# The output projection of the second attention stage in half arrays, its loads and stores by GpSimd, and a new order of its steps

## The chip, the cores and the metric

The kernel runs on one core of a Trainium2 chip. A core has a matrix engine (TensorE, PE in the profile; its weight loads are PEld), VectorE (DVE), ScalarE (ACT), GpSimd (POOL) and SyncE (SP), which here only issues DMA transfers. Time is the device time of one execution in microseconds, the median of several runs.

## The reference: what is computed

A sequence of 2048 tokens of width 576 passes through two layers, and each layer is an attention block and a gated mixer block, both with a residual connection:

```python
x = x + _A_ref(_layernorm(x), A_wqkv, A_wo)
x = x + _B_ref(_layernorm(x), B_w_in, B_w_sp, B_b_sp, B_w_out)
```

and the same two lines once more with the same weights. The attention has 32 heads of width 18; a token attends to eight tokens, itself and those 2, 4, ... 14 positions before it. Its result goes through the output projection `A_wo` (576 x 576), which this case is about. The mixer computes `z = gelu(x @ w_in)` of width 4608, normalises the second half (called z2 here) over its width, mixes it over the tokens with `w_sp` (2048 x 2048), adds a bias, multiplies by the first half (z1) and projects back with `w_out`. Inputs and output are bf16.

## The kernel before

The program runs five phases: F (attention of layer one, and z2 of its mixer), S (token mixing), F again (first the output projection of the first mixer, called p3, then the attention of layer two and its z2), S again, and E (the last output projection). The second F is `phase_F` with `first` false; in it TensorE, VectorE, ScalarE, GpSimd and SP work on many small steps side by side.

The tokens are worked on in 16 blocks of 128 rows (index i) for p3, W and z2, in 18 attention tiles of 114 rows (index t), since a tile of 128 keys serves 114 queries, and in six groups of three tiles (index g) for Q and K. The steps of the second F are:

- `p3_steps`: for block i, 36 matmuls (L491) with `w_out`, the residual sum on VectorE (L536), and LayerNorm (`ln_steps`): statistics on VectorE (L416, L417), three small steps on GpSimd (L421 to L424), normalisation on ScalarE (L437), and a transposing DMA on SP into `xnD` (L454).
- `QK_steps`, `V_steps`: projections of Q and K (L395, L401, L720), which SP's DMAs write into `QK`, and of V (L754).
- `ATT_steps`: for tile t, logits (L792), exponential on ScalarE (L799), mask on VectorE (L806), the product with V (L814), the division by the sum on VectorE (L822, L823) into `o_t`, a transposing DMA on SP (`turned`, L849), and a copy into `oT` by VectorE or ScalarE (`ev`, L471 or L472). `o_t` has two buffers.
- `W_steps`: for block i, the output projection of the attention (L880), the residual sum (L536), the store of the row block to DRAM, and the LayerNorm before the mixer, the steps called y.
- `Z2_steps`: the z2 part of `w_in` for block i (L914 and L921 on TensorE), gelu on ScalarE (L937), sums of squares and normalisation on VectorE (L949, L988). Its weights come by ten DMAs, the steps `win2.k`, made in `win2_parts`.

Width 576 is four chunks of 128 rows and 64 more. The contraction over these 64 is done in two ways. `mm576` (L387) runs eight full matmuls for two results and then, or before them, two matmuls of 64 rows, one in the upper and one in the lower half of the array, with the operands lying on partitions 0 to 63 for the one and 64 to 127 for the other. Q and K and z2 work like that. The output projection instead takes five chunks for each half of its columns, where the fifth is filled with zeros: in the second F `o_tb` has 64 columns of zeros behind the 576, and rows 64 to 127 of the last chunk of `wo` are zeros, both written by GpSimd in `fill`.

Nobody writes the order of the steps by hand. Each step is registered with `fl.step(name, engine, cost, key, function, after, uses, takes, mode, pairs)`. `Flow.order` then plays the engines with these costs: of the steps that could begin first on an engine it takes the one with the lowest key. Keys are made of the tile or block number and the numbers in `PLANS`: KX ranks p3, KQ the projections of Q and K, KV those of V, KL the logits, KE the exponentials, KM the masks, KP the product with V, KF the division, KO the transposing DMA of `o_t`; KY ranks the LayerNorm after W, KZ and KS rank z2 (KZ + KS times the block). STAY is a bonus for staying in the same mode. A mode is the way that TensorE's array is divided: "w" full, "n" halves of 64 rows, "c" and "h" halves of columns, "q" quarters of rows; "wn" begins with the one in which TensorE is and ends in the other. The plan thus fixes the order on every engine before the kernel starts, and on the chip each engine works through its list in order and waits on semaphores.

Row stores and z2 weight loads go to the queue that is named `side`, L586:

```python
side, SIDE = (nc.gpsimd, ("POOL", 0.66)) if first else (nc.sync, ("SP", 0.5))
```

A load `win2.k` may be issued when the logits of tile 11 + k // 2 have been given to TensorE and all p3 blocks are through (L1108).

Of the kernel before, what the change touches and what calls it, by code (L numbers as in the profile page):

```python
# [20 lines left out]
P = 128  # L21
HP = 64
S = 2048
D = 576
FH = 2304
H = 32
# [14 lines left out]
NM = D // P  # L41
# [11 lines left out]

Plan = namedtuple("Plan", "LX LW LR KQ KX KV KL KE KM KP KF KY KZ KS STAY LF KO", defaults=(0,))
PLANS = (Plan(LX=4, LW=3.41, LR=2.6, KQ=3.82, KX=5.34,
              KV=1.52, KL=21.62, KE=163.6, KM=20.74, KP=31.25, KF=55.71, KY=7.57, KZ=169.61, KS=25.3, STAY=1.61, LF=4.38, KO=17.77),
         Plan(LX=5.14, LW=3.5, LR=2.6, KQ=6.48, KX=9.99,
              KV=3.68, KL=12.54, KE=0, KM=0, KP=11.94, KF=53.62, KY=74.68, KZ=0, KS=32.42, STAY=8.78, LF=3.89, KO=6.42))
SCALE = DH ** -0.5


# [208 lines left out]
class K:  # L270
# [270 lines left out]
    def phase_F(self, li):  # L541
        nc, tc = self.nc, self.tc
        first = li == 0
# [10 lines left out]
        pl = PLANS[0 if first else 1]  # L554
        fl = Flow(dict(QK=NQK[ly], stg=NSTG[ly], stx=NSTX[ly], xt=NX, xn=3, ln_st=6, o_t=2, oq=2), pl.STAY, self.pairs, pl.LF,
                  0.8 if first else 0.0, first)
# [9 lines left out]
        wo = att.tile([P, 5, D], bf16, name="wo")  # L566
# [4 lines left out]
        oT = att.tile([P, 5, RING], bf16, name="oT")  # L571
        o_tb = [att.tile([P, D if first else D + HP], bf16, name=f"o_t{k}") for k in range(2)]
        oq = [self.zu[:, 0, a:a + 5 * P].rearrange("p (c n) -> p c n", n=P) for a in (0, 2176)]

        def x_tile(i):
            if i < NXZ:
                return self.zu[:, NB, D * i:D * (i + 1)]
            return xts[i - NXZ][:]
# [4 lines left out]
        def x_held(i):  # L583
            return [b for _, b in x_takes(i)]
        win2a = self.wA[:].rearrange("p (c s t) n -> p c s (t n)", c=NM - 1, s=2)
        side, SIDE = (nc.gpsimd, ("POOL", 0.66)) if first else (nc.sync, ("SP", 0.5))  # L586
        win2b = wB[:]
        win2r = wC[:]

# [61 lines left out]
        def load_o():  # L651
            eng = nc.sync
            self.dma(wo[:, 0:4, :], self.A_wo[0:512, :].rearrange("(c p) n -> p c n", p=P), eng)
            self.dma(wo[HP:P, 4, :] if first else wo[0:HP, 4, :], self.A_wo[512:576, :], eng)

# [117 lines left out]
        def ATT_steps(t, key):  # L775
            v, box, Psb = vb[t % 3], {}, Pb[t % 2]
# [3 lines left out]
            tag = f"a{t}"  # L780
# [37 lines left out]
            def fin(_):  # L818
                o_t = box["o"] = o_tb[t % 2][:, 0:D]
                O = box["O"][:, :, 0:16 * (DH + 1)].rearrange("p s (h e) -> p s h e", e=DH + 1)  # L820
                rec = att.tile([P, 2, 16], f32, name="rec", bufs=2)
                nc.vector.reciprocal(out=rec[:], in_=O[:, :, :, DH])  # L822
                nc.vector.tensor_tensor(out=o_t.rearrange("p (s h d) -> p s h d", s=2, d=DH), in0=O[:, :, :, 0:DH],  # L823
                                        in1=rec[:, :, :, None].to_broadcast([P, 2, 16, DH]), op=ALU.mult)
            landed = [f"qk{group[t]}.w{d}" for d in range(NM // 2 + 1)] + ([f"qk{group[t]}.h"] if group[t] else [])
            both = [("H", tag + ".L0"), ("H", tag + ".L1")]
            if first:
# [2 lines left out]
            else:  # L830
                fl.step(tag + ".L", "PE", 0.62, key - pl.KL, lambda _: Lm(0, True), landed, [f"QK{group[t]}"], takes=both, mode="q", pairs=2 * H)
            fl.step(tag + ".x0", "ACT", 0.9, key - pl.KE, ex(0), [tag + (".M" if first else ".L"), "fill"] + ([f"a{t - 2}.v"] if t > 1 else []), [tag + ".L0"],
                    mode="x")
            fl.step(tag + ".x1", "ACT", 0.9, key - pl.KE, ex(1), [tag + ".x0"], [tag + ".L1"], mode="x")
            fl.step(tag + ".k", "DVE", 1.07, key - pl.KM, mk, [tag + ".x1", "masks"])
            fl.step(tag + ".v", "PE", 0.54 if first else 0.53, key - pl.KP, pv, [tag + ".k", f"v{t}.e0", f"v{t}.e1"] + ([f"ones{t}"] if t < 3 else []) + ([f"a{t - 1}.v"] if t else []),
                    takes=[("H", tag + ".O")], mode="c", pairs=H)
            fl.step(tag + ".f", "DVE", 1.11, key - pl.KF, fin, [tag + ".v"], [tag + ".O"], takes=[("o_t", f"o_t{t}")])
            n = min(QT, S - QT * t)

            def tr(_):
# [27 lines left out]
        def W_steps(i):  # L869
            box, g, rows = {}, f"w{i}", slice(P * i, P * i + P)  # L870
            t_of = range(P * i // QT, min(NT - 1, (P * i + P - 1) // QT) + 1)
            key = t_of[-1]
            at = P * i % RING

            def wm(hh):
                def f(_):
                    if hh == 0:
                        box["ps"] = self.Ht()
                    for c in range(5):
                        nc.tensor.matmul(box["ps"][:, hh, 0:288], lhsT=oT[:, c, at:at + P],  # L880
                                         rhs=wo[:, c, hh * 288:(hh + 1) * 288], start=(c == 0), stop=(c == 4))
                return f

            def add(_):
                self.add_x(x_tile(i), box["ps"], x_tile(i))

            def store(_):
                self.dma(self.xres[0 if first else 1][rows, :], x_tile(i), side)
            fl.step(g + ".m0", "PE", 0.61, key, wm(0), [f"a{t}.e" for t in t_of] + ["wo", "fill"], takes=[("H", g + ".ps")], mode="w", pairs=5)
            fl.step(g + ".m1", "PE", 0.61, key, wm(1), [g + ".m0"], [g + ".ps"], mode="w", pairs=5)  # L890
            fl.step(g + ".a", "DVE", 0.73, key, add, [g + ".m1", ("lnx" if first else "p3_") + f"{i}.n"], [g + ".ps", *x_held(i)])
            fl.step(g + ".w", *SIDE, key, store, [g + ".a"], x_held(i), lag=pl.LW)
            users = [t for t in range(NT) if QT * t - HALO < P * (i + 1) and P * i < QT * t + QT]
            guard = [f"v{t}.m" for t in users]
            guard += [f"qk{gg}.m{d}" for gg in sorted({group[t] for t in users}) for d in range(5)]
            self.ln_steps(fl, f"y{i}", key + pl.KY, P * i, lambda: x_tile(i), [g + ".a"], x_held(i), guard)
# [140 lines left out]
        def fill(_):  # L1037
            for k in range(2):
                nc.gpsimd.memset(Pb[k][:, :, :, QH:HP], 1.0)
            nc.gpsimd.memset(wo[0:HP, 4, :] if first else wo[HP:P, 4, :], 0.0)  # L1040
            if not first:
                for k in range(2):
                    nc.gpsimd.memset(o_tb[k][:, D:], 0.0)

        def ones(k):
            def f(_):
# [20 lines left out]
        if first:  # L1067
            fl.step("wv", "SP", 1.4, -18, lambda _: load_v(), lag=6.0)
        fl.step("wo", "SP", 0.9, -17, lambda _: load_o(), ["wv", "qk1.w1"] if first else [], lag=4.0)
        z = "DVE" if first else "POOL"  # L1070
        zero = nc.vector if first else nc.gpsimd
# [4 lines left out]
        for k in range(3):  # L1076
            fl.step(f"vzero{k}", z, 0.6, -4 if first else -12, lambda _, k=k: zero.memset(vbi[k][:], 0), ["lnx1.p"] if first else [])
            fl.step(f"ones{k}", "POOL", 0.5, -3 if first else -15, ones(k), [f"vzero{k}"])
        fl.step("fill", "POOL", 1.5, -40, fill)
        fl.step("masks", "POOL", 2.0, -16, lambda _: self.masks() if first else None)  # L1080
        if first:
# [8 lines left out]
            for k, (n, cost, pre) in enumerate(((9, 5.15, []), (3, 0.95, ["lnx0.t", "spin0"]), (2, 0.6, ["lnx1.t", "spin1"]))):  # L1090
                fl.step(f"spin{k}", "PE", cost, -100, turn(n), pre, ["spin"] if k else [],
                        takes=[] if k else [("H", "spin")], mode="w", pairs=n)
        for i in range(NS):
            g = next(g for g in range(len(sizes)) if QT * (t0s[g] + sizes[g]) > P * i)
# [6 lines left out]
        for t in range(NT):  # L1101
            V_steps(t, t - pl.KV)
        for t in range(NT):
            ATT_steps(t, t)
        for i in range(NS):
            W_steps(i)
# [6 lines left out]
        if first:  # L1113
            made = [f"wqk{b}" for b in range(NM)] + [f"ends{k}" for k in range(4)] + ["wqk_r", "wv"]
# [807 lines left out]
```

## Time and profile before

| what | us |
|---|---|
| median of 3 runs | 1105.55 (1104.48 to 1106.67) |
| profiled execution, its time | 1105.93 |
| its span, first to last instruction | 1104.2 |
| first F, about | 0 to 200 |
| first S | 200 to 489 |
| second F | 489 to 749 |
| second S and E | 749 to 1104 |

The mean clock that TensorE was granted is 0.998 of full speed. The answers of the profile that are quoted below have these forms. A row of a stretch lists its length, then the busy time and number of instructions of PE, PEld, DVE, ACT and POOL, the granted clock, the mean busy share of the 16 DMA engines, and GB/s. A row of waits reads: who waited, for whom, us in total, times, the longest. A row of the order of time begins with start and duration in us; in square brackets stands how long the engine had been idle before it, and what ended that. A group has its count behind an x, then busy us and the mean ns of one. A row of one line's instructions has minimum, median and maximum ns. SPq is an issue on SP's queue; a DMA row ends with the us from issue to landing.

### The profile page before, as it was taken

To read this page: it belongs to the slowest core of one execution; us is meant where nothing else is said; L and a number is where in the kernel's file an instruction comes from. 1 tells how busy PE (TensorE), PEld (TensorE's weight loads), DVE (VectorE), ACT (ScalarE), POOL (GpSimd) and SP (SyncE) were. 2 spreads that over 40 slices of the span, in tenths; PEclk is the share of its full clock that TensorE was granted. 3 is DMA by queue.
4 is the path that set the end of the run, shared out by engine and by line. 5 is a ranking of instruction groups with operands and counts; after the bars stand their busy time and mean duration, and the time that the engine had idled before them with its cause. 6 is when DMAs were issued, how large, how long until landed. Compare 5 with 4: busy or idle time off the path is not lost. (4 is left out here: it accounts for less than half of the span.)

```text
span 1104.2 us, 24979 instructions
## 1 busy us (share of the span) xinstructions
PE 1088.9 (99%) x10249; PEld 621.8 (56%) x10249; DVE 801.6 (73%) x1442; ACT 518.2 (47%) x744; POOL 231.9 (21%) x456
## 2 busy tenths in 40 slices
PE   8999999999999999999999999999999999999998
PEld 5777655444444444457777765554444444444586
DVE  8898888987777677854566788467766676676686
ACT  7788898832221422202465578873122214323250
POOL 6354548411111001122111124530000000000000
PEclk9999999999999999999999999999999999999999
DMA  7877580587769625573344496602122192211421
GB/s 190 169 143 167 133 177 1 150 204 247 226 199 335 207 84 158 165 249 93 73 73 79 95 187 151 245 1 61 36 60 60 40 358 67 60 49 57 175 81 54
DMA packets 192586, 147.96 MB, mean 134 GB/s; under 512 B 145784, under 2 KB 174584, under 8 KB 188760
## 3 DMA queue, kind: packets, MB, share of 16 engines
q1 hardware_dynamic: 182616, 105.92, 37.7%
q0 software_dynamic: 9856, 40.45, 11.1%
q8 instruction: 80, 1.31, 0.5%
q14 instruction: 34, 0.28, 0.1%
HBM read 77.78 MB, written 37.92 MB: 105 GB/s over the span
## 5 line engine op out<-in xcount | busy, mean ns | idle before, releaser
L1303 ACT ACTIVATE zu<-psum 128x1024 bf16<-128x1024 f32 x72 | 73.3, 1021 | 332.9 <-PE psum L1299 292.3
L1318 PE MATMUL psum<-S,T 128*128 128x512 f16 x856 | 198.8, 379 | 0.0
L1318 PEld LDWEIGHTS <-T 128*128 128x128 f16 x1144 | 111.9, 98 | 125.8 <-issue 0.2
L1370 DVE SCALAR_TENSOR_TENSOR g<-psum,wsc,bsp 128x512 f32<-128x512 f32 (+1 forms) x130 | 97.4, 750 | 83.8 <-PE psum L1318 82.4
L1291 PE MATMUL psum<-xnD,w 128*128 128x512 bf16 x576 | 136.4, 380 | 0.0
L914 PE MATMUL psum<-wA,xnD 128*128 128x384 bf16 x576 | 109.7, 327 | 0.3 <-DVE v_ext L471 0.2
L1318 PEld LDWEIGHTS <-zu 128*128 128x128 bf16 x640 | 62.6, 98 | 73.0 <-issue 0.5
L914 PEld LDWEIGHTS <-xnD 128*128 128x128 bf16 x768 | 72.0, 98 | 56.0 <-issue 11.9
L1291 PEld LDWEIGHTS <-w 128*128 128x128 bf16 x576 | 53.4, 98 | 71.1 <-issue 15.3
L1370 DVE SCALAR_TENSOR_TENSOR g<-psum,wsc,g 128x512 bf16<-128x512 f32 (+1 forms) x93 | 66.0, 710 | 36.3 <-PE psum L1318 34.5
L937 ACT ACTIVATE zu<-psum 128x768 bf16<-128x768 f32 x96 | 76.9, 804 | 22.5 <-PE psum L921 20.0
L1318 PE MATMUL psum<-A,zu 128*128 128x512 bf16 x352 | 82.0, 379 | 0.0
L949 DVE CUSTOM_DVE_ANT_1 zu<-zu 128x1536 bf16<-128x1536 bf16 x28 | 49.1, 1752 | 27.1 <-ACT zu L937 26.7
L799 ACT ACTIVATE P<-psum 128x912 bf16<-128x912 f32 x72 | 64.0, 942 | 9.4 <-PE psum L792 6.6
L1318 PE MATMUL psum<-S,zu 128*128 128x512 f16 x288 | 68.0, 379 | 0.3 <-DVE g L1370 0.3
L1318 PE MATMUL psum<-A,T 128*128 128x512 bf16 x288 | 68.0, 379 | 0.0
L401 PE MATMUL psum<-xnD,wqkv 128*128 128x228 bf16 (+1 forms) x480 | 64.9, 280 | 2.3 <-DVE wqkv L623 1.5
L491 PEld LDWEIGHTS <-zu 128*128 128x128 bf16 x576 | 56.1, 98 | 14.7
L1330 DVE TENSOR_TENSOR zu<-g,zu 128x512 bf16<-128x512 bf16 x129 | 54.9, 425 | 8.7
L401 PEld LDWEIGHTS <-wqkv 128*128 128x128 bf16 x480 | 43.7, 97 | 16.7 <-issue 7.6
L437 ACT ACTIVATE xn<-zu,ln_st 128x512 bf16<-128x512 bf16 (+1 forms) x52 | 31.1, 647 | 46.4 <-POOL ln_st L424 46.2
L491 PE MATMUL psum<-wA,zu 128*128 128x288 bf16 x384 | 52.6, 286 | 0.0
(209 smaller groups left out, 1786.4 us busy)
## 6 DMA issues: line engine op xcount, KB each, us to landing
w<-in_B_w_in_dram SPq DMA_DIRECT2D x72, 128.0 KB, 2.5
ustore<-zu POOLq DMA_DIRECT2D x18, 512.0 KB, 3.6
zu<-ustore SPq DMA_DIRECT2D x18, 512.0 KB, 4.2
S<-op SPq DMA_DIRECT2D x8, 1024.0 KB, 13.8
A<-op SPq DMA_DIRECT2D x6, 1024.0 KB, 11.1
wA<-in_B_w_out_dram SPq DMA_DIRECT2D x12, 432.0 KB, 4.2
QK<-stg SPq DMA_DIRECT2D x36, 114.0 KB, 3.9
QK<-stg SPq DMA_DIRECT2D x24, 171.0 KB, 3.7
```

What stands on the lines that cost most here:

```text
L401: nc.tensor.matmul(ps(s), lhsT=lhsT, rhs=rhs, start=(c == 0 and not rest_first), stop=(c == NM - 1 and rest_first))
L437: nc.scalar.activation(out=out, in_=in_, func=ACT.Identity, scale=rstd[:n], bias=nmr[:n])
L491: nc.tensor.matmul(ps[:, hh, 0:288], lhsT=u[:, s * S + i * P:s * S + (i + 1) * P], rhs=wout(b, s)[:, hh * 288:(hh + 1) * 288], start=(b == ...
L799: nc.scalar.activation(out=Psb[:, 2 * hh:2 * hh + 2, :, 0:QH], in_=box["L", hh][:, :, 0:8 * QH].rearrange("p a (b c) -> p a b c", c=QH), f ...
L914: nc.tensor.matmul(box[u][:, s, 0:384], lhsT=self.xnD[:, c, at], rhs=(win2a[:, c, s] if c < NM - 1 else win2b[:, s])[:, cols], start=(firs ...
L937: nc.scalar.activation(out=self.zu[:, 3 * u + 1:3 * u + 4, 256 * i:256 * (i + 1)].rearrange("p j (s r) -> p s j r", s=2), in_=box[u][:, :, ...
L949: nc.vector.tensor_tensor_reduce(out=junk(0, 6), in0=z[:, 0:6, :], in1=z[:, 0:6, :], scale=1.0 / FH, scalar=0.0, op0=ALU.mult, op1=ALU.add ...
L1291: nc.tensor.matmul(ps[:, h, :], lhsT=w1[:, NM * h + d, :], rhs=self.xnD[:, d, t0:t0 + 512], start=(opens and d == 0), stop=(not opens and ...
L1303: nc.scalar.activation(out=u_of(jj, c)[:, :, 512 * k:512 * k + 512], in_=ps, func=ACT.Gelu_apprx_tanh)
L1318: nc.tensor.matmul(ps, lhsT=lhs[:, i, :], rhs=rhs[:, i, :], start=(opens and i == 0), stop=(i == 7), skip_group_check=not opens)
L1330: nc.vector.tensor_tensor(out=uv, in0=g, in1=uv, op=ALU.mult)
L1370: nc.vector.scalar_tensor_tensor(out=out, in0=ps, scalar=inv[c], in1=other, op0=ALU.mult, op1=ALU.add)
```

## The change

It has four parts, all in the second F; the first F keeps its form.

1. The output projection of a block becomes one step in the manner of `mm576`: eight full matmuls and two of 64 rows in the two halves of the array (`halves`), with mode "wn". For this the last 64 rows of `wo` are loaded twice, to both halves of the partitions (`load_o`), and VectorE copies the last 64 columns of `o_t` behind the 576 (`fin`), so that the transposing DMA delivers them on both halves. The zeros in `fill` go.
2. The row stores and the z2 weight loads are issued by GpSimd instead of SP (`side`).
3. The costs in the plan follow: 1.1 for W as one step, 1.21 for the division with the copy.
4. The numbers of the second plan are new, and so the order of all steps of the second F.

```diff
-         Plan(LX=5.14, LW=3.5, LR=2.6, KQ=6.48, KX=9.99,
-              KV=3.68, KL=12.54, KE=0, KM=0, KP=11.94, KF=53.62, KY=74.68, KZ=0, KS=32.42, STAY=8.78, LF=3.89, KO=6.42))
+         Plan(LX=5.14, LW=3.5, LR=2.6, KQ=6.06, KX=9.99, KV=2.42, KL=11.66, KE=10.56, KM=-1.95, KP=11.34, KF=71.99, KY=260.04, KZ=0, KS=0.84, STAY=8.35, LF=3.89, KO=0.46))
...
-        side, SIDE = (nc.gpsimd, ("POOL", 0.66)) if first else (nc.sync, ("SP", 0.5))
+        side, SIDE = nc.gpsimd, ("POOL", 0.66)
...
-            self.dma(wo[HP:P, 4, :] if first else wo[0:HP, 4, :], self.A_wo[512:576, :], eng)
+            for k in (1,) if first else (0, 1):
+                self.dma(wo[HP * k:HP * k + HP, 4, :], self.A_wo[512:576, :], eng)
...
+                if not first:
+                    nc.vector.tensor_copy(out=o_tb[t % 2][:, D:D + HP], in_=o_t[:, D - HP:D])
...
-            fl.step(tag + ".f", "DVE", 1.11, key - pl.KF, fin, [tag + ".v"], [tag + ".O"], takes=[("o_t", f"o_t{t}")])
+            fl.step(tag + ".f", "DVE", 1.11 if first else 1.21, key - pl.KF, fin, [tag + ".v"], [tag + ".O"], takes=[("o_t", f"o_t{t}")])
...
+            def halves(rest_first):
+                ps = box["ps"] = self.Ht()
+                cols = [slice(288 * hh, 288 * hh + 288) for hh in range(2)]
+                self.mm576(lambda hh: ps[:, hh, 0:288], rest_first,
+                           lambda hh, c: (oT[:, c, at:at + P], wo[:, c, cols[hh]]),
+                           lambda hh, rows: (oT[rows, NM, at:at + P], wo[rows, NM, cols[hh]]))
...
-            fl.step(g + ".m0", "PE", 0.61, key, wm(0), [f"a{t}.e" for t in t_of] + ["wo", "fill"], takes=[("H", g + ".ps")], mode="w", pairs=5)
-            fl.step(g + ".m1", "PE", 0.61, key, wm(1), [g + ".m0"], [g + ".ps"], mode="w", pairs=5)
+            made = [f"a{t}.e" for t in t_of] + ["wo"]
+            if first:
+                fl.step(g + ".m0", "PE", 0.61, key, wm(0), made + ["fill"], takes=[("H", g + ".ps")], mode="w", pairs=5)
+                fl.step(g + ".m1", "PE", 0.61, key, wm(1), [g + ".m0"], [g + ".ps"], mode="w", pairs=5)
+            else:
+                fl.step(g + ".m1", "PE", 1.1, key, halves, made, takes=[("H", g + ".ps")], mode="wn", pairs=10)
...
-            nc.gpsimd.memset(wo[0:HP, 4, :] if first else wo[HP:P, 4, :], 0.0)
-            if not first:
-                for k in range(2):
-                    nc.gpsimd.memset(o_tb[k][:, D:], 0.0)
+            if first:
+                nc.gpsimd.memset(wo[0:HP, 4, :], 0.0)
```

## The prediction

> **What bounds the kernel now.** I read the page first, then the busy times by stretch, then who TensorE waited for, and last the order of time around its longest wait.
>
> ```profile
> span 1104.2 us, 24979 instructions
> PE 1088.9 (99%) x10249; PEld 621.8 (56%) x10249; DVE 801.6 (73%) x1442; ACT 518.2 (47%) x744; POOL 231.9 (21%) x456
> ```
>
> TensorE is busy 99% of the span, so only two things can shorten the kernel: less TensorE work, or less of the 1% in which it stands still or runs at a lower clock. The second attention stage (first L491 matmul at 489.44, last z2 matmul at about 749) is the only stage whose order the change touches.
>
> ```profile
> core 0: us, PE busy (x) PEld busy (x) DVE busy (x) ACT busy (x) POOL busy (x), PEclk, DMA share, GB/s
> 489.40:537.00 47.60, 47.60 (x375) 35.88 (x374) 19.26 (x39) 10.46 (x18) 16.59 (x41) 1.00 0.44 112
> 537.00:600.00 63.00, 62.40 (x1135) 45.14 (x1133) 40.72 (x67) 36.55 (x54) 9.81 (x26) 1.00 0.35 69
> 640.00:650.00 10.00, 10.00 (x228) 6.58 (x233) 8.69 (x18) 7.39 (x12) 2.42 (x6) 1.00 0.91 199
> 656.00:658.00 2.00, 2.00 (x51) 1.62 (x51) 1.64 (x4) 1.40 (x3) 0.13 (x1) 1.00 1.46 33
> 658.00:662.00 4.00, 1.94 (x25) 0.83 (x26) 1.66 (x3) 2.01 (x4) 0.00 (x0) 0.86 0.87 175
> 662.00:666.00 4.00, 4.00 (x146) 2.94 (x146) 2.80 (x9) 3.18 (x5) 1.05 (x3) 0.72 0.70 173
> 700.00:749.00 49.00, 49.00 (x320) 26.08 (x318) 29.03 (x39) 36.97 (x85) 16.59 (x39) 1.00 0.19 54
> 489.00:749.00 260.00, 254.84 (x3585) 171.23 (x3584) 164.48 (x277) 157.46 (x281) 74.15 (x172) 0.99 0.49 114
> ...
> PE psum L880 <- ACT oT L472: 2.1, 1, 2.1
> ```
>
> Over the whole stage (the last stretch) TensorE stands still for 260.00 - 254.84 = 5.2 us, with nothing of it before 537 or after 700. The longest wait, 2.1 us on the copy into oT by ScalarE (L472), is followed by a lower clock. The third number from the right is the granted clock: 1.94 x (1 - 0.86) + 4.00 x (1 - 0.72) = 0.27 + 1.12 = 1.4 us is lost there. So 5.2 + 1.4 = 6.6 us is the most that fewer waits can win, and more than half of it (2.1 + 1.4) hangs on one wait. Its causes, in order of time:
>
> ```profile
> 651.28 2.12 SPq L286 DMA_DIRECT2D wA<-in_B_w_in_dram  x2
> 653.50 1.23 SPq L849 DMA_TRANSPOSE zu<-o_t  x1
> 655.58 2.44 SPq L849 DMA_TRANSPOSE zu<-o_t  x1
> 659.94 0.74 ACT L472 COPY oT<-zu 128x570 bf16<-128x570 bf16 x1 [2.54 <-DMA zu<-o_t]
> 660.01 0.76 DVE L823 TENSOR_TENSOR o_t<-psum,rec 128x576 bf16<-128x576 f32 x1 [1.86 <-DMA zu<-o_t]
> 660.73 1.30 PE L880 MATMUL psum<-wo,oT 128*128 128x288 bf16 x5 [2.06 <-ACT oT L472]
> ...
> DMA to landing us min/median/max: 2.6/2.8/3.8
> wA<-in_B_w_in_dram SPq DMA_DIRECT2D x2, 288.0 KB, 5.4
> ```
>
> Two z2 weight loads go out on SP at 651.28, the transposing DMA of an attention output right behind them at 653.50. The median of such a transpose (L849) is 2.8 us to landing; this one is read only at 659.94, which is 6.4 us. Meanwhile ScalarE, VectorE and then TensorE stand still. The two loads, issued on the same queue, needed 5.4. In 656 to 658 the DMA engines are counted as more than fully busy (1.46) while they move 33 GB/s. So the wait is a transfer queued behind others, not arithmetic.
>
> **The change part by part.** *The output projection (W).* TensorE now does ten matmuls for a block of 128 rows, five row chunks for each of two column halves, the fifth chunk padded with zeros. After the change there are eight full ones and two of 64 rows, which lie in two halves of the array.
>
> ```profile
> 578.71 2.61 PE L880 MATMUL psum<-wo,oT 128*128 128x288 bf16 x20 [0.32 <-ACT v_ext L472]
> 581.16 1.63 PE L491 MATMUL psum<-wA,zu 128*128 128x288 bf16 x12
> ...
> 710.93 1.15 PE L914 MATMUL psum<-wA,xnD 128*128 128x384 bf16 x6
> 712.24 1.14 PE L914 MATMUL psum<-wA,xnD 128*128 128x384 bf16 x6
> 714.94 0.66 PE L921 MATMUL psum<-wC,xnD 64*128 64x384 bf16 x6
> 715.53 1.15 PE L914 MATMUL psum<-wA,xnD 128*128 128x384 bf16 x6
> ```
>
> Twenty W matmuls (two blocks) take 581.16 - 578.71 = 2.45 us, so one takes 0.1225 and a block 1.225. The price of the new form is read from z2, which has it already: eight full matmuls take 712.24 - 710.93 = 1.31 us, or 0.164 each. From 710.93 to 715.53 there are 24 of them and three pairs of halves. If a pair takes the time of one full matmul, that is 27 x 0.164 = 4.42; measured are 4.60, and the 0.18 left are two changes between full and half rows, some 0.09 each. So a new W block takes 9 x 0.1225 = 1.10, and 0.09 for the change inside it: 1.19 against 1.225, a gain of 0.035, or 16 x 0.035 = 0.55 us in all. That holds where a block stands between steps of other forms, as in nearly all of the present order, and for two blocks in a row. Bounds: between neighbours that already end and begin in half rows, no extra change is paid, 16 x 0.1225 = 2.0 us gained; a lone block between two full-row steps pays two, 16 x (0.18 - 0.1225) = 0.9 us lost. I take 0.4 gained, nearest to the middle case.
>
> The Trainium skill, TensorEngine Tiling (Array Packing), Key Properties, says that a change of tiling mode drains TensorE, which speaks against this edit; its speedup table would by itself give up to 2x on the last chunk. By the table alone the gain would be 2.0, by the rows above it is 0.55; the 0.09 us per change is what the drain costs here.
>
> *The copy of the last 64 columns.* It replaces a fill with zeros, since the halves need the last 64 rows of the transposed output on both halves of the partitions: 18 copies of 128x64 on VectorE, between the division (L823) and the transposing DMA.
>
> ```profile
> L471 DVE COPY oT<-zu 128x60 bf16<-128x60 bf16 x1 | 0.2, 197 | 0.6 <-DMA zu<-o_t 0.6
> L961 DVE TENSOR_TENSOR zst<-zst 128x2 f32<-128x2 f32 x2 | 0.3, 157 | 0.0
> ```
>
> Between 0.157 and 0.197 us each, 3 us of VectorE in all, and as much later for each transpose. VectorE has 22.3 of 63 us free in 537 to 600, but only 1.3 of 10 in 640 to 650. I charge those that fall where it is tight, six of the 18, with half of their 0.18: 0.5 us on the path; none at best, 18 x 0.197 = 3.5 at worst. The fills with zeros that go from GpSimd, and the one more DMA for the second copy of the last rows of wo (an issue on SP ahead of the loads of x, about 0.5 us as the others below), lie beside 47.60 us of unbroken TensorE work: nothing. Without that cover they would cost 0.5 us once.
>
> *Loads and stores from SP to GpSimd.* Ten loads of z2 weights and sixteen row stores leave SP's queue, and each becomes an instruction of GpSimd:
>
> ```profile
> L286 SPq DMA_DIRECT2D xres<-xt x9: 319/429/576, 637.9 to 686.6; - x9
> L286 SPq DMA_DIRECT2D wA<-in_B_w_in_dram x6: 409/550/1747, 635.1 to 653.0; - x6
> L286 POOL DMA_DIRECT2D xres<-xt x9: 539/632/646, 85.1 to 136.0; - x9
> L286 POOL DMA_DIRECT2D wA<-in_B_w_in_dram x6: 546/590/794, 34.9 to 79.4; - x6
> wA<-in_B_w_in_dram POOLq DMA_DIRECT2D x6, 288.0 KB, 4.0
> wA<-in_B_w_in_dram SPq DMA_DIRECT2D x6, 288.0 KB, 4.4
> ```
>
> SP loses 16 x 0.43 + 10 x 0.55 = 12.4 us of issuing, most of it in 580 to 690, where it also gives out every transpose (L849, L454) and every write of Q and K. GpSimd gains 16 x 0.63 + 10 x 0.59 = 16 us; it is busy 2.42 of 10 us in 640 to 650. The loads land no later from there (4.0 against 4.4). A load waits for the logits of tile 11 to 15; behind a waiting load on GpSimd stand the small LayerNorm steps (L421 to L424), ScalarE's normalisation (L437) waits for these, then SP's transpose, then z2.
>
> What it is worth hangs on the waits above. The first attention stage issues the same loads and stores from GpSimd already; its table:
>
> ```profile
> 50.00:75.00 25.00, 24.68 (x602) 18.84 (x599) 22.03 (x47) 18.63 (x31) 13.46 (x30) 1.00 0.70 141
> 75.00:100.00 25.00, 25.00 (x618) 19.69 (x615) 22.34 (x45) 23.14 (x38) 13.56 (x28) 1.00 0.69 150
> 100.00:125.00 25.00, 24.47 (x593) 18.05 (x591) 21.32 (x40) 19.57 (x30) 9.60 (x18) 1.00 0.69 157
> ```
>
> There TensorE stands still 0.32 + 0 + 0.53 = 0.85 us in 75, at full clock. Over the 135 us from 537 to 672 that would be 1.5 us: the good end. The bad end is no relief, 5.2. I take the middle, 3.4 us left, because the loads keep their trigger and so can still meet the transposes on the DMA engines; that saves 1.8, and with the 2 us wait shortened the dip of the clock goes as well, 1.4.
>
> *The order anew.* New ranks let other steps run first: z2 all close together (KS 0.84), the LayerNorm after W last (KY 260), the exponentials earlier (KE). What TensorE has to do is not altered; z2 is the same 48 units. No row prices an order that has not run. Its bounds are those of the idle time, 6.6 us won to another such wait with its dip, 2.1 + 1.4 = 3.5 us lost; I take 0 beyond what is booked above.
>
> **The sum.** -0.4 (W) + 0.5 (copies) - 1.8 (idle) - 1.4 (clock) = -3.1 us. The profiled execution took 1105.93 (its span 1104.2 and 1.7 around it), 0.4 above the median of 1105.55, so its sum is 1102.8, and on the median 1102.4.
>
> **The rivals.** *The jam stays (no change).* The ten loads still follow the logits of tiles 11 to 15, two for each, and go through the same DMA engines, whose share was 0.91 in 640 to 650 and 1.46 in 656 to 658 whoever issued. For it: the late transpose had been issued in 1.23 us and was late in flight. Against it: stage one. The stall and the dip then stay, W and copies cancel: 1105.55 - 0.4 + 0.5 = 1105.7.
>
> *GpSimd becomes the late engine (slower).* Its queue is in order. In the stretch 640 to 670 it would get some six loads and six stores, 6 x 0.59 + 6 x 0.63 = 7.3 us, ahead of LayerNorm steps that have to be through before z2 can fill TensorE at 669. For it are steps that were stretched beside VectorE:
>
> ```profile
> 113.29 1.71 POOL L424 TENSOR_SCALAR ln_st<-ln_st 128x1 f32<-128x1 f32 x1
> 113.75 1.11 DVE L806 TENSOR_TENSOR P<-P,maskT 128x1824 bf16<-128x1824 bf16 x1
> ```
>
> Against it: of the GpSimd issues above none took over 0.794. It decides once GpSimd's free 7.6 us in ten are filled at the hand-over to z2. If half of the 7.3 us is late and the wait there brings its own dip of 1.4: 1105.55 + 3.7 + 1.4 - 0.4 = 1110.2; with a quarter late and no dip, 1107.0.
>
> The Trainium skill, SBUF — State Buffer, section "SBUF: two separate sides", warns of that: while VectorE is in a two-port mode GpSimd cannot write descriptors, and a 620 ns issue was seen to take 3100. By it 26 issues would cost up to 26 x 2.5 = 65 us of GpSimd; the rows of stage one (at most 0.794) do not bear it out, so I give it no more than this rival's chance.
>
> *The order alone wins more.* All idle time falls to stage one's 1.5 us and W finds half-row neighbours: 3.7 + 1.4 + 2.0 = 7.1 us won, 1098.4.
>
> **How the numbers follow.** The forecast (gain between 1.2 and 5) gets 0.48, the jam that stays 0.18, GpSimd late or another new wait 0.24, the large gain 0.10. A run tells 0.2%, about 2.2 us, from no change. Three quarters of the forecast's chance lie beyond that bound (0.36), with the large gain (0.10) and a third of the jam's, since the order may win elsewhere (0.06): faster 0.52. Slower is the GpSimd rival less its mild end (0.20) and another third of the jam's (0.06): 0.26. What is left is the same: 0.12 + 0.04 + 0.06 = 0.22. The predicted time is 1102.4. The range goes from the large gain, 1098.4, past the mild end of the slower rival to 1108.2; the forecast's own range is 1100.5 to 1104.4.
>
> **What would show it.** Right: no wait of TensorE on oT (L472) over 1 us, and no stretch with a granted clock below 1.00 between 640 and 670; the L849 transposes land within 3.8 us; the W block followed by the next step in 1.19 us instead of 1.225; GpSimd's issues about 0.6 us. Wrong: idle time of TensorE in the stage at 5 us or more, waits on ln_st (L424) or xnD at the start of z2, or new waits in 489 to 537 and after 700, where now there are none. The prediction fails above all if the new order opens a wait at a place where the old one had none.

## The result, and the profile after

The changed kernel takes 1114.51 us (median of 6 runs, 1112.19 to 1117.69) against 1105.28 (6 runs) before: a ratio of 1.0077 with a 95% interval of 1.0061 to 1.0093. It is slower; forecast was 1102.4, in a range that ended at 1108.2.

The page of the changed kernel, its span and the busy time of each engine:

```profile
span 1114.4 us, 24981 instructions
PE 1092.8 (98%) x10249; PEld 621.5 (56%) x10249; DVE 808.3 (73%) x1473; ACT 511.8 (46%) x731; POOL 248.4 (22%) x479
```

The second F now runs from its first p3 matmul at 490.67 to the first z1 matmul of the next phase at 759.06, 268.39 us; before it ran from 489.44 to 749.04, 259.60 us. The stage is 8.8 us longer. The rest of the span's 10.2 us is 1.2 by which the stage begins later, and 0.2 behind it. The stretches of the stage in the changed kernel (length, busy PE, PEld, DVE, ACT, POOL, then granted clock, share of the DMA engines, GB/s):

```profile
490.67:759.06 268.39, 257.05 (x3583) 169.76 (x3582) 171.30 (x307) 150.99 (x269) 89.94 (x195) 0.97 0.52 110
645.00:649.00 4.00, 0.87 (x65) 0.66 (x50) 1.82 (x3) 0.70 (x2) 0.12 (x1) 0.85 1.24 179
649.00:652.00 3.00, 3.00 (x13) 1.14 (x12) 0.00 (x0) 2.84 (x4) 0.00 (x0) 0.50 0.84 177
652.00:656.00 4.00, 4.00 (x20) 1.98 (x20) 2.33 (x3) 0.73 (x1) 0.00 (x0) 0.67 0.33 72
748.00:752.00 4.00, 0.02 (x1) 0.02 (x2) 2.33 (x3) 1.33 (x4) 0.00 (x0) 0.77 1.05 353
752.00:756.00 4.00, 4.00 (x13) 1.92 (x14) 0.00 (x0) 0.00 (x0) 0.00 (x0) 0.50 0.17 28
756.00:760.00 4.00, 4.00 (x24) 1.78 (x22) 0.74 (x1) 2.43 (x6) 0.00 (x0) 0.87 0.00 0
```

TensorE stands still for 268.39 - 257.05 = 11.3 us, where it was 5.2. Behind each of two stalls it works at half the clock: 3.00 x 0.50 + 4.00 x 0.33 + 4.00 x 0.50 + 4.00 x 0.13 = 5.3 us lost, where it was 1.4. Together that is 6.1 + 3.9 = 10.0 us more, 1.2 above what the stage grew by; ends of matmuls are modelled, and the clock is averaged over my cuts, so I take no more from this than that the two stalls with their clock hold the whole loss. The waits of TensorE in the stage, the longest first:

```profile
PE psum L927 <- DMA xnD<-xn: 4.5, 1, 4.5
PE psum L792 <- issue: 3.1, 1, 3.1
PE psum L394 <- DVE oT L470: 1.2, 1, 1.2
```

The wait of 2.1 us on oT, the longest before, is gone from its place; an output projection now waits 1.2 us on oT at 670. Two new waits are longer. I call them **stall A** (L792, at 645) and **stall B** (L927, the last block of z2, at 747).

**Stall A**, in order of time, TensorE of the changed kernel:

```profile
643.49 1.42 PE L754 MATMUL psum<-wqkv,xnD 128*64 128x288 bf16 x20 [0.49 <-ACT P L799]
644.84 0.60 PE L792 MATMUL psum<-QK 32*64 32x57 bf16 x52
648.57 0.32 PE L792 MATMUL psum<-QK 32*64 32x57 bf16 x12 [3.13 <-issue]
648.83 2.46 PE L400 MATMUL psum<-xnD,wqkv 128*128 128x342 bf16 x8
```

TensorE stops at 645.44, after 52 of the 64 matmuls of one step. "issue" means that it waited for nothing the profile shows, so for no operand either. The eight matmuls behind it take 2.46 us. GpSimd at that time:

```profile
637.44 0.63 POOL L285 DMA_DIRECT2D wA<-in_B_w_in_dram  x1 [0.21 <-PE psum L814]
638.07 0.55 POOL L285 DMA_DIRECT2D wB<-in_B_w_in_dram  x1
...
641.42 0.54 POOL L285 DMA_DIRECT2D wC<-in_B_w_in_dram  x1
641.94 0.57 POOL L285 DMA_DIRECT2D wA<-in_B_w_in_dram  x1
...
643.94 1.17 POOL L285 DMA_DIRECT2D wA<-in_B_w_in_dram  x2
```

Six z2 weight loads go out in 7.7 us, and in 645 to 649 the DMA engines are counted as more than full (1.24 above).

**Stall B**, the queue of SP in the changed kernel, then TensorE's wait:

```profile
708.59 3.11 SPq L851 DMA_TRANSPOSE zu<-o_t  x2
725.27 1.20 SPq L453 DMA_TRANSPOSE xnD<-xn  x1
726.52 5.60 SPq L285 DMA_DIRECT2D A<-op_A  x2
732.99 1.23 SPq L453 DMA_TRANSPOSE xnD<-xn  x1
734.32 2.77 SPq L285 DMA_DIRECT2D S<-op_S  x4
737.13 0.43 SPq L285 DMA_DIRECT2D A<-op_A  x1
737.72 2.88 SPq L453 DMA_TRANSPOSE xnD<-xn  x1
740.71 8.72 SPq L285 DMA_DIRECT2D w<-in_B_w_in_dram  x4
```

```profile
730.39 1.14 PE L400 MATMUL psum<-wo,oT 128*128 128x288 bf16 x8
...
751.98 2.10 PE L927 MATMUL psum<-wA,xnD 128*128 128x384 bf16 x6 [4.53 <-DMA xnD<-xn]
...
DMA to landing us min/median/max: 14.2/14.2/14.2
```

The last transpose into xnD is issued at 737.72, behind seven loads of 1 MB each (the token mixing matrices A and S of the next phase). It lands 14.2 us later, and the last z2 block reads it at 751.98. The same queue before:

```profile
684.18 0.38 SPq L286 DMA_DIRECT2D A<-op_A  x1
684.91 1.64 SPq L454 DMA_TRANSPOSE xnD<-xn  x1
...
687.75 1.96 SPq L286 DMA_DIRECT2D S<-op_S  x4
689.75 0.43 SPq L286 DMA_DIRECT2D A<-op_A  x1
691.91 10.49 SPq L454 DMA_TRANSPOSE xnD<-xn  x2
...
DMA to landing us min/median/max: 15.0/15.0/15.0
```

The plan puts the seven loads behind the last output projection (`blocks`, L1132), since their buffers are opened where the attention's are given up; on the chip the first goes out at 726.52 and the other six from 731.79, when the last projection (begun at 730.39) is through. With the old order the loads began at 684; the last transpose behind them, begun at 694.1, landed 15.0 us later as well, but z2 still ran for 40 us beyond that. With the new rank of z2 (KS 0.84 for 32.42), z2 blocks come ahead of the last attention tiles: their transposes go out at 708.59, the last W block runs at 730.39, and the loads come together with the last transposes, when too little z2 is left to cover these.

### The profile page after: what moved, and what is told of

It is laid out like the page before. It is cut to its first block, busy times and chain, and to the rows that moved or that the text cites. A ratio compares the mean times of both kernels' runs of the same rounds, so it can differ in the third digit from the quotient of the medians.

```text
span 1114.4 us, 24981 instructions
## 1 busy us (share of the span) xinstructions
PE 1092.8 (98%) x10249; PEld 621.5 (56%) x10249; DVE 808.3 (73%) x1473; ACT 511.8 (46%) x731; POOL 248.4 (22%) x479
## 3 DMA queue, kind: packets, MB, share of 16 engines
q8 instruction: 80, 1.31, 0.5%
## 5 line engine op out<-in xcount | busy, mean ns | idle before, releaser
L927 PE MATMUL psum<-wA,xnD 128*128 128x384 bf16 x576 | 111.6, 331 | 4.8 <-DMA xnD<-xn 4.5
L927 PEld LDWEIGHTS <-xnD 128*128 128x128 bf16 x768 | 72.5, 99 | 62.5 <-issue 14.6
L400 PE MATMUL psum<-xnD,wqkv 128*128 128x228 bf16 (+1 forms) x480 | 67.2, 287 | 1.9 <-DVE wqkv L622 1.2
L436 ACT ACTIVATE xn<-xt,ln_st 128x512 bf16<-128x512 bf16 x72 | 42.9, 646 | 23.4 <-POOL ln_st L423 23.4
```

The lines of the kernel that those rows point to most:

```text
L400: nc.tensor.matmul(ps(s), lhsT=lhsT, rhs=rhs, start=(c == 0 and not rest_first), stop=(c == NM - 1 and rest_first))
L927: nc.tensor.matmul(box[u][:, s, 0:384], lhsT=self.xnD[:, c, at], rhs=(win2a[:, c, s] if c < NM - 1 else win2b[:, s])[:, cols], start=(firs ...
```

## The experiments

The theory after the result had two parts: stall A belongs to the z2 loads on GpSimd's queue, and stall B to the rank of z2. Rivals were that any new order would do this, that the halves of the array or the copies cost more than thought, and that GpSimd as an engine was late. The table holds the ratio to before with its interval, and from the one profiled execution of each the length of the stage, first p3 matmul to first z1 matmul.

| kernel | ratio | interval | stage, us |
|---|---|---|---|
| before | 1 | | 259.60 |
| changed | 1.0077 | 1.0061 to 1.0093 | 268.39 |
| halves_only | 0.9998 | 0.9982 to 1.0015 | 259.28 |
| order_only | 1.0080 | 1.0050 to 1.0109 | 267.64 |
| pool_only | 1.0076 | 1.0051 to 1.0101 | 270.69 |
| gpsimd_same_order | 1.0044 | 1.0021 to 1.0068 | 264.77 |
| loads_gpsimd | 1.0022 | 1.0006 to 1.0038 | 259.84 |
| stores_gpsimd | 1.0013 | 0.9999 to 1.0027 | 258.16 |
| new_order_sp | 1.0028 | 1.0014 to 1.0042 | 262.41 |
| no_win2 | 1.0020 | 1.0004 to 1.0035 | 261.79 |
| old_ks | 1.0015 | 1.0005 to 1.0025 | 261.29 |
| ops_late | 1.0114 | 1.0094 to 1.0133 | 270.32 |
| old_ks_sp | 0.9978 | 0.9967 to 0.9990 | 256.85 |
| win2_early | 1.0044 | 1.0027 to 1.0060 | 264.83 |

A ratio is that of whole executions, and the first F, which is the same in all these kernels, brings some chance into it. In the profiled execution of order_only TensorE stood still there, inside one output projection:

```profile
50.56 1.15 PE L879 MATMUL psum<-wo,oT 128*128 128x288 bf16 x5 [4.49 <-issue]
```

At the same instruction it paused 2.85 us in the profiled executions of gpsimd_same_order and of no_win2 and 2.02 in that of loads_gpsimd, and not at all in those of before, changed and old_ks_sp. Half clock follows the three longest of these pauses, so the second F begins at 495.68, 495.12 and 493.94 instead of 489.44. The length of the stage is free of this, but it comes from one execution of each kernel.

### The parts alone

**halves_only**: the changed kernel with the old numbers of the plan and loads and stores by SP, so that only the halves, the copies and the second load of the last rows of wo are left.

```diff
-         Plan(LX=5.14, LW=3.5, LR=2.6, KQ=6.06, KX=9.99, KV=2.42, ... KS=0.84, STAY=8.35, LF=3.89, KO=0.46))
+         Plan(LX=5.14, LW=3.5, LR=2.6, KQ=6.48, KX=9.99, KV=3.68, ... KS=32.42, STAY=8.78, LF=3.89, KO=6.42))
-        side, SIDE = nc.gpsimd, ("POOL", 0.66)
+        side, SIDE = (nc.gpsimd, ("POOL", 0.66)) if first else (nc.sync, ("SP", 0.5))
```

> The new output projection and its copies alone; plan numbers and SP queue as before (the order shifts a little, since the step costs differ). Theory A (the time is lost by the new order, where the last LayerNorm transposes of z2 stand behind the 7 MB of operator loads, and where TensorE's instructions come late beside the z2 weight loads): 1104 to 1106.5, W blocks 1.19 us. Rival B (half arrays and copies cost the time): 1108 or more. Rival C (GpSimd's queue is late): as theory A.

Ratio 0.9998, 0.9982 to 1.0015: no change that can be told. The rival that the halves or the copies cost the 9 us is ruled out.

**order_only**: the kernel before with the new numbers of the plan, nothing else.

```diff
-         Plan(LX=5.14, LW=3.5, LR=2.6, KQ=6.48, KX=9.99, KV=3.68, ... KS=32.42, STAY=8.78, LF=3.89, KO=6.42))
+         Plan(LX=5.14, LW=3.5, LR=2.6, KQ=6.06, KX=9.99, KV=2.42, ... KS=0.84, STAY=8.35, LF=3.89, KO=0.46))
```

> The new plan numbers alone; old projection, SP queue. Theory A: 1110 to 1115, with a wait of 3 to 5 us on xnD among the last z2 blocks, since two operator loads still stand ahead of the last transposes but one. Rivals B and C: 1104 to 1107.

Ratio 1.0080. TensorE's two longest waits are 6.0 us on xnD (stall B) and 3.5 us on oT; in this stage there is none of the kind of stall A. The new order alone loses about as much as the whole change, in the stage (8.0 us of 8.8) as in the ratio, whose interval is wide.

**pool_only**: the kernel before with `side` as in the change. The planner is told that the steps run on GpSimd, so the order changes as well.

```diff
-        side, SIDE = (nc.gpsimd, ("POOL", 0.66)) if first else (nc.sync, ("SP", 0.5))
+        side, SIDE = nc.gpsimd, ("POOL", 0.66)
```

> Loads and stores by GpSimd alone; old projection, old plan numbers. Theory A: 1101 to 1106.5, the last LayerNorm transposes still land in time. Rival B: within 1104 to 1106. Rival C: 1108 or more, with TensorE waiting for work that hangs on GpSimd.

Ratio 1.0076, so this part alone loses as much too, and not the 1101 to 1106.5 of theory A. The longest waits of TensorE in that kernel are in other places, and none is for a step of GpSimd, as rival C had it:

```profile
PE psum L814 <- ACT v_ext L472: 3.3, 1, 3.3
PE psum L792 <- DMA QK<-stx: 2.0, 1, 2.0
```

A pause of 1.4 us on "issue" (L792) comes on top. Since two things change here, the queue and the order that the planner makes for it, the next run keeps them apart.

### The queue

**gpsimd_same_order**: the kernel before, planned as before, so that every engine keeps its order; only the issuing of the ten loads and sixteen stores goes to GpSimd.

```diff
-        side, SIDE = (nc.gpsimd, ("POOL", 0.66)) if first else (nc.sync, ("SP", 0.5))
+        side, SIDE = (nc.gpsimd, ("POOL", 0.66)) if first else (nc.gpsimd, ("SP", 0.5))
```

> The kernel before with loads and stores of the second attention stage issued by GpSimd, but planned as if by SP: the order on every engine stays that of the kernel before, only the queue differs. Theory Q (the queue itself costs: from their own queue the z2 weight loads run beside the transposes and TensorE's instructions instead of between them): 1108 to 1114, with L849 transposes of over 5 us to landing. Theory O (only the planner's other order costs): 1103 to 1107.

Ratio 1.0044: the queue alone costs something, but how much is loosely known. The interval goes from 0.21% to 0.68%; two of the ten executions, near 1118 us, raise the ratio, and the medians differ by 2.7 us (1108.86 and 1106.21). The profiled execution is one of the two, and part of its excess is the pause in the first F. The landing of the transposes of o_t (L849) in this kernel, in us as minimum, median and maximum; then VectorE, then TensorE at the longest wait:

```profile
DMA to landing us min/median/max: 3.8/6.1/8.4
```

```profile
652.92 0.58 DVE L471 COPY oT<-zu 128x60 bf16<-128x60 bf16 x2 [4.17 <-DMA zu<-o_t]
...
653.79 0.76 DVE L823 TENSOR_TENSOR o_t<-psum,rec 128x576 bf16<-128x576 f32 x1
```

```profile
654.60 0.76 PE L792 MATMUL psum<-QK 32*64 32x57 bf16 x62 [3.58 <-DVE o_t L823]
```

The trace gives a landing for only two of the 18 transposes, 8.4 us for the one issued at 644.5 and 3.8 for one at 663.4; before, it gave four, 2.6/2.8/3.8. So the medians say little, but the waits show the old jam again, and longer: a transpose is late, the copies into oT hold up VectorE, the division behind them is late, and TensorE waits for the psum tile that it frees. Moving the loads off SP's queue did not keep this transpose from being late in flight. The Trainium skill, DMA: Bandwidth & Descriptors, section "SWDGE vs HWDGE vs iDMA", says that the queues fed by GpSimd and by SP are different and that an engine takes turns between them; the landing of 8.4 us agrees with that, but no run here shows the turns.

**loads_gpsimd** and **stores_gpsimd**: the same, for the ten loads alone and for the sixteen stores alone.

```diff
-                    out.append(lambda _, dst=dst, src=self.B_w_in[r0:r1, cols]: self.dma(dst, src, side))
+                    out.append(lambda _, dst=dst, src=self.B_w_in[r0:r1, cols]: self.dma(dst, src, nc.gpsimd))
```

```diff
-                self.dma(self.xres[0 if first else 1][rows, :], x_tile(i), side)
+                self.dma(self.xres[0 if first else 1][rows, :], x_tile(i), nc.gpsimd)
```

> The kernel before, same order, with only the ten z2 weight loads issued by GpSimd and the sixteen stores left on SP. If the loads carry the cost of the queue: 1107.5 to 1111, as gpsimd_same_order. If the stores do: 1104.5 to 1106.5.

> The kernel before, same order, with only the sixteen stores issued by GpSimd. If the loads carry the cost: 1103.5 to 1106.5. If the stores do: 1107.5 to 1111.

1.0022 and 1.0013; together 0.35% against the 0.44% of both at once. The stores' interval reaches 0.9999, and in the profiled executions neither stage is much longer than before (259.84 and 258.16). Both medians (1107.01 and 1107.28) lie between the ranges that were to tell the two apart, so how the cost divides between loads and stores stays open.

**new_order_sp**: the changed kernel, in its own order, with the issuing back on SP.

```diff
-        side, SIDE = nc.gpsimd, ("POOL", 0.66)
+        side, SIDE = (nc.gpsimd, ("POOL", 0.66)) if first else (nc.sync, ("POOL", 0.66))
```

> The changed kernel with its order on every engine, but the loads and stores issued by SP. Theory Q: the stall at 645 with a wait for nothing the profile shows (3.1 us) and the low clock behind it shrink, the wait for xnD of 4.5 us stays: 1107 to 1112. Theory O: 1112 to 1117 with both stalls.

Ratio 1.0028: 0.49%, or 5.4 us, of the loss is gone. TensorE's longest waits:

```profile
PE psum L927 <- DMA xnD<-xn: 4.4, 1, 4.4
PE psum L792 <- issue: 0.8, 1, 0.8
```

Stall A is down from 3.1 to 0.8 us; stall B is untouched.

**no_win2**: the changed kernel without the ten z2 loads of the second F. They are left out, and z2 of layer two works on what lies in the tiles; no other step is altered.

```diff
-                    out.append(lambda _, dst=dst, src=self.B_w_in[r0:r1, cols]: self.dma(dst, src, side))
+                    out.append((lambda _, dst=dst, src=self.B_w_in[r0:r1, cols]: self.dma(dst, src, side)) if first else (lambda _: None))
```

> The changed kernel, same order, without the ten loads of z2 weights in the second attention stage (z2 then works on what lies in those tiles). If these loads are what makes TensorE's instructions and the transposes late at 645, that stall (3.1 us and 3 us of low clock) goes and only the wait on xnD stays: 1106 to 1110. If the transposes do it by themselves, the stall stays: 1112 to 1116.

Ratio 1.0020. The place of stall A in this kernel:

```profile
648.30 0.60 PE L792 MATMUL psum<-QK 32*64 32x57 bf16 x52
649.32 0.25 PE L792 MATMUL psum<-QK 32*64 32x57 bf16 x12 [0.41 <-issue]
649.50 1.34 PE L400 MATMUL psum<-xnD,wqkv 128*128 128x342 bf16 x8
```

The pause stands behind the same 52 matmuls, 0.41 us long, and the eight behind it take 1.34 us instead of 2.46. So the length of stall A comes from the loads. What TensorE waits for can be read from one more queue. The page has it, here of the changed kernel:

```profile
q8 instruction: 80, 1.31, 0.5%
```

It lists packets, MB and share. 1.31 MB in 80 packets is 16.4 KB each, and TensorE's 10249 matmuls and 10249 weight loads, 20498 in all, are 256 for each packet; so I take these packets for TensorE's instructions. The Trainium skill, Runtime: NRT & Kernel Launch, section "Instruction fetch mechanics", says that an engine's instructions are fetched by DMA in blocks of 16 KiB, 256 instructions, while the block before is worked on, and that the cost is mostly hidden. The size agrees. The records of these packets, set beside TensorE's pause behind the 52nd matmul in six kernels of this order (us from the start of the span):

| kernel | z2 loads | L754 step begins | packet begins | packet ends | pause | TensorE goes on |
|---|---|---|---|---|---|---|
| old_ks_sp | SP | 641.94 | 641.55 | 643.04 | 0.51 | 644.41 |
| no_win2 | none | 646.95 | 647.08 | 648.04 | 0.41 | 649.32 |
| new_order_sp | SP | 642.54 | 642.81 | 643.82 | 0.82 | 645.32 |
| old_ks | GpSimd | 642.58 | 643.21 | 644.13 | 1.08 | 645.62 |
| ops_late | GpSimd | 644.11 | 645.26 | 646.35 | 1.91 | 647.98 |
| changed | GpSimd | 643.49 | 645.89 | 647.22 | 3.13 | 648.57 |

The pause stands at the same place of the program in all six, and ends 1.3 to 1.6 us behind the packet's end in all six. The packet takes about the same time in each (0.9 to 1.5 us); it begins between 0.4 us ahead of the start of the L754 step and 0.3 us behind it with the loads left out or on SP, and 0.6 to 2.4 us behind it with the loads on GpSimd. In the changed kernel TensorE had already stopped when it began; in the other five it began 0.8 to 2.4 us before the stop. So stall A is a block of TensorE's own instructions that came late because its transfer began late, while the z2 loads from GpSimd were under way. The delay is not the same each time: with the same loads on GpSimd the pause was 1.08, 1.91 and 3.13 us, each in one execution. Why the same loads from SP let the packet begin in time no record shows.

### The order

**old_ks**: the changed kernel with the old rank of z2.

```diff
-         Plan(LX=5.14, LW=3.5, LR=2.6, ... KY=260.04, KZ=0, KS=0.84, STAY=8.35, LF=3.89, KO=0.46))
+         Plan(LX=5.14, LW=3.5, LR=2.6, ... KY=260.04, KZ=0, KS=32.42, STAY=8.35, LF=3.89, KO=0.46))
```

> The changed kernel with KS as before (32.42): z2 ranks behind the last attention tiles again, W of the last blocks and with it the operator loads come before most of z2. If the late W and the late 7 MB of loads are the second cause, the wait for xnD goes without a new one at the hand-over: 1105 to 1110. If not, 1112 or more.

Ratio 1.0015: 0.62%, or 6.9 us, of the loss is gone. The seven loads go out from 683.75 to 697.53 (684.18 to 690.18 before the change), and no wait on xnD is left. What is left, a wait of 2.7 us at L720 on a copy of VectorE and the pause of 1.08 us, is the queue's share: with the issuing back on SP too (old_ks_sp below) that wait is gone and the pause is 0.51 us.

**ops_late**: the changed kernel, but the loads of A and S may not be issued until the last transpose into xnD is through.

```diff
-        fl.step("blocks", "SP", 0.0, 900, lambda _: self.open_blocks(li + 1, acm), [f"w{i}.m1" for i in range(NS)])
+        fl.step("blocks", "SP", 0.0, 900, lambda _: self.open_blocks(li + 1, acm), [f"w{i}.m1" for i in range(NS)] + ([] if first else [f"y{i}.e" for i in range(NS)]))
```

> The changed kernel, with the operator loads of the token mixing planned behind the last LayerNorm transpose. Theory A: the wait of 4.5 us on xnD and the low clock behind it go, 5 to 8 us less than the changed kernel, 1106 to 1110; a new wait of token mixing on its operators may give back 1 to 4. Rivals B and C: 1113 or more, since the wait comes from elsewhere.

Ratio 1.0114, worse. TensorE behind the last z2 block in this kernel:

```profile
751.60 0.49 PE L927 MATMUL psum<-wB,xnD 128*128 128x384 bf16 x2
761.35 0.61 PE L1302 MATMUL psum<-xnD,w 128*128 128x512 bf16 x1 [9.26 <-DMA w<-in_B_w_in_dram]
```

The wait on xnD is gone, so the seven loads had caused it. But now the loads of w, which come behind them on SP's queue (742.88), are late for the next phase, and TensorE stands still for 9.26 us in place of 4.53. Seven MB that start only around 730 were late for somebody in either place of the queue. That it is the early end of the attention which is missing is shown by old_ks, which has it back.

**old_ks_sp**: both undone, the old rank of z2 and the issuing on SP; the halves, the copies and the other new ranks stay.

```diff
-         Plan(LX=5.14, LW=3.5, LR=2.6, ... KY=260.04, KZ=0, KS=0.84, STAY=8.35, LF=3.89, KO=0.46))
+         Plan(LX=5.14, LW=3.5, LR=2.6, ... KY=260.04, KZ=0, KS=32.42, STAY=8.35, LF=3.89, KO=0.46))
-        side, SIDE = nc.gpsimd, ("POOL", 0.66)
+        side, SIDE = (nc.gpsimd, ("POOL", 0.66)) if first else (nc.sync, ("POOL", 0.66))
```

> The order of old_ks on every engine (half arrays, all new plan numbers but KS), with loads and stores issued by SP. If the late operator loads and GpSimd's z2 loads are the two causes and nothing else in the new order costs, both are gone here: 1101 to 1105.5, a ratio to before of 0.996 to 1.000. If something else in the order costs too: 1106.5 or more.

1103.37 us, ratio 0.9978 with an interval of 0.9967 to 0.9990: faster than both kernels. TensorE's longest waits, and the whole stage:

```profile
PE psum L792 <- ACT v_ext L471: 1.1, 1, 1.1
```

```profile
489.00:749.00 260.00, 255.62 (x3600) 169.11 (x3598) 172.30 (x312) 155.68 (x277) 72.77 (x170) 1.00 0.55 115
```

4.4 us idle in 260 (5.2 before the change), and no stretch at a lower clock. The two repairs win 6.0 and 7.1 us of the stage by themselves and 11.5 together: two losses that nearly add up. Which of the new ranks that stay wins the 2.5 us over the kernel before was not run.

**win2_early**: another way to keep the loads from the transposes, tried on the kernel before: all ten may go out behind the logits of tile 10.

```diff
-            fl.step(f"win2.{k}", *SIDE, 0, f, [f"a{3 + k if first else min(11 + k // 2, NT - 1)}.L"] +
+            fl.step(f"win2.{k}", *SIDE, 0, f, [f"a{3 + k if first else 10}.L"] +
```

> The kernel before with all ten z2 weight loads allowed after the logits of tile 10 (the last p3 block still ends first), so they go out together at about 625 on SP. If the jam of loads and transposes at 650 to 660 is what holds the kernel before, its 2.1 us wait and the low clock go: 1100 to 1104. If transposes jam by themselves or the burst meets others: 1105 to 1110.

Ratio 1.0044, slower. The planner moves other steps too, and the longest waits are new ones, 1.3 to 1.5 us on the division (L823) and on gelu (L937).

This miss says nothing on the loads by themselves; it is one more order that was worse than the one it replaced.

## Why the prediction was wrong

**The output projection, -0.4 us: not contradicted.** Two blocks in a row in the changed kernel:

```profile
604.90 1.15 PE L400 MATMUL psum<-wo,oT 128*128 128x288 bf16 x8
605.98 0.42 PE L394 MATMUL psum<-wo,oT 64*128 64x288 bf16 x4
...
607.42 0.70 PE L792 MATMUL psum<-QK 32*64 32x57 bf16 x64
```

607.42 - 604.90 = 2.52 us, or 1.26 for a block, where the full fifth chunk took 2.56 for two at the same place (602.10 to 604.66); in the other pair, from 573.73 to 576.16, it is 2.43 against 2.45. That is 0.01 to 0.02 us for a block, below the 0.035 that I took, and 16 of them are below what halves_only could resolve (0.9982 to 1.0015, or 2.0 us won to 1.7 lost). A block so takes 1.22 to 1.26 us, longer than the 1.19 named as the sign of a right step: the direction holds, the size was too large.

**The copies, +0.5 us: not contradicted.** The 18 copies take 0.181 to 0.200 us each, inside the 0.157 to 0.197 read from other copies but for the longest; what they put on the path stays in halves_only's interval too.

**Loads and stores to GpSimd, -1.8 and -1.4 us: wrong in sign.** This step failed. It argued from the first stage, where the same loads from GpSimd left 0.85 us of idle time in 75. Its table began at 50; the loads begin at 34.9, and the stretch left out is worse:

```profile
25.00:50.00 25.00, 23.49 (x612) 18.32 (x610) 22.12 (x41) 19.51 (x31) 8.41 (x19) 1.00 0.92 176
```

With it the good end would have been (1.51 + 0.85) / 100 x 135 = 3.2 us instead of 1.5. And this was one execution: in those of order_only, gpsimd_same_order, no_win2 and loads_gpsimd the same first stage had a pause on "issue" of 2.0 to 4.5 us, so the quiet rows of before were luck. In the first stage, besides, six loads of wA are spread over 34.9 to 79.4; in the changed second stage six z2 loads go out in 7.7 us. With every engine in its old order the move costs 0.44% (0.21% to 0.68%; 2.7 us by the medians), and in the changed order 5.4 us, where I had 3.2 won. The prediction had seen that "the late transpose had been issued in 1.23 us and was late in flight", and gave this to the rival that the jam stays. That was the right reading: in gpsimd_same_order a transpose was late in flight with the loads off SP's queue too. (The typical landing of 2.8 us beside it came from four of the 18 transposes.) No row of before had a pause on "issue" over 0.3 us, so stall A was not foreseen.

**The order anew, 0 us: wrong, with the loss beyond its bound.** By itself it costs 0.80% (8.8 us, with an interval from 5.5 to 12; the stage grew by 8.0), where the bound was 3.5, "another such wait with its dip". In the changed kernel it costs 6.9 us by the rank of z2 alone. The step counted what TensorE has to do, which is the same, and did not follow what else waits for the end of the attention: the seven loads of the next phase, which are steps of SP and not in the diff. The profile before showed it already: the last transpose took 15.0 us to land behind them, and nobody waited only since z2 still ran for 40 us. "z2 all close together" was named as what the ranks do; what z2 then stands ahead of was the question left out.

**The rivals.** *GpSimd becomes the late engine* had the right sign and the wrong mechanism. Its issues take 0.54 to 0.67 us, no longer than in the first stage, and no wait on the small LayerNorm steps is among the longest. The Trainium skill, SBUF — State Buffer, section "SBUF: two separate sides", warns that a DMA issued by GpSimd can be stretched from 620 to 3100 ns beside VectorE. No issue of GpSimd here is stretched like that. *The jam stays* was half right: a transpose is still late in flight where only the queue changes (8.4 us). *The order alone wins more* is contradicted by order_only. The last sentence of the prediction, that a new order opening a wait where there was none would break it, is what happened, twice; its chance was set too low.

## What to carry to other kernels

A new rank is costed by what it makes late for the next phase: look in the profile for transfers that land late without anyone waiting, and ask which work covers them and whether the new order still puts it there. Moving DMA issues to another queue saves that queue's time; here it did not help a transfer that had been issued in time and was late in flight, and it delayed another, that of TensorE's instructions. A quiet stretch of one profile is one execution: look at the same stretch in other runs before taking it as a price. Where several parts of a change are independent, run them alone and then without the losing ones: here the best kernel was the change without its move of the queue and without one number of its plan.

## What the runs showed of the hardware

- A DMA queue that the profile counts on the same 16 engines as the data carried 80 packets of 16.4 KB, one for every 256 of TensorE's matmuls and weight loads. In six kernels TensorE paused at the same instruction and went on 1.3 to 1.6 us after such a packet had ended. The packet began 0.6 to 2.4 us behind a fixed step with the z2 loads on GpSimd's queue, and within 0.4 us of it without them there; the longest pause was 3.13 us.
- Such a pause varies between executions of the same steps: in the first F it was 4.49, 2.85, 2.85 and 2.02 us in four profiles, and absent in others.
- Before the change, eight of the nine transposes into xnD whose landing the trace gives took 2.6 to 5.2 us; the one behind 7 MB of loads took 15.0. In the changed kernel such a one took 14.2.
- In the clock records of these traces TensorE's clock is half behind a stall for 3.41 us, 6.83 us or once 10.24 us: 3.41 before the change (after a wait of 2.1), 6.83 twice in the second F of the changed kernel (after 3.1 and 4.5), 10.24 in ops_late (after 9.3). The wait of 4.4 us in new_order_sp was followed by 3.41 us, that of 4.6 in no_win2 by 6.83, so the length of the wait alone does not say which.
